# Another order of the value products in a windowed-attention section: four phases of 320 columns, heads alternating between the two halves

## The chip, the cores and the metric

One core of one Trainium2 chip runs the whole program in one launch. The metric is device time in microseconds (us). Several runs of the kernel before were timed; one more execution was recorded by the hardware profiler, and its page and trace are what is read here. Engine names are those of the profile: PE is TensorE's matmul, PEld its weight load, DVE is VectorE, ACT is ScalarE, POOL is GpSimd, SP is SyncE.

## The reference

A gate mixes an attention branch and a feed-forward branch over the same input, with 2048 positions and 512 features:

```
def A(x, wqkv, wo):                        # x: 1 x 2048 x 512
    H = 32; Dh = 16; W = 256
    q, k, v = split(x @ wqkv)              # 32 heads of 16
    scores = einsum("bhqd,bhkd->bhqk", q, k) * Dh ** -0.5
    mask = (i - j >= 0) & (i - j < W)      # causal, window of 256
    p = softmax(where(mask, scores, -1e9))
    return einsum("bhqk,bhkd->bhqd", p, v) @ wo
def B(x, w_gate, w_up, w_down):            # 512 -> 1792 -> 512
    return (silu(x @ w_gate) * (x @ w_up)) @ w_down
g = sigmoid((x * gate_w).sum(-1, keepdims=True))
out = g * A(x) + (1 - g) * B(x)
```

## The kernel before

The 32 heads are worked on in G = 8 groups g of four heads j. Positions come in 16 blocks of 128 (the block of keys is called kb) and in 4 chunks c of 512 columns (the queries). The program has three stretches: projections and first scores (to about 95 us), the attention groups with the feed-forward's gate and up products between them (about 95 to 603 us), and the down products and the output (to the end).

In the attention stretch the loop at L694 runs over slots t, each with four steps hd. A step issues, in a fixed order, one matmul of the next group's scores (`stage1`, L302, reduced to a row maximum on DVE at L304), one transposed score of this group (`stage2`, L344, turned by ACT's Exp at L346 into the probabilities `pt`, which POOL masks at L348 and L351), and six feed-forward matmuls (L252). Once in four slots, in the step hd == 1 of part 0, it calls `av(ag, c)` (L715), the section that is changed, and then `finish(ag, c)`, whose first instruction is ACT's copy at L383, followed by DVE's sum and transposes. All of it is ordered by hand: every engine takes its instructions in the order of the program, and waits are put in where data or a buffer is needed.

A section `av(g, c)` makes, for one group and one chunk, the products of values and probabilities and, by a column of ones, their sums. Both operands are fp32; one matmul call of the program becomes two weight loads and two matmul passes on PE. A block of 128 keys is split by `HALVES` into its first and last 64 keys, so that TensorE's rows are used as two halves h: half 0 reads partitions 0 to 63 and sums into one PSUM tile (`pb`, or `pa` at the very end), half 1 reads partitions 64 to 127 and sums into another (`ps`). The four heads write 32 partitions each. So eight places of the array, two halves by four heads, can work beside each other.

What a block gives to a chunk depends on where it lies. With m the block's number relative to the chunk's first block, the columns of the product are:

| m | -2 | -1 | 0 | 1 | 2 | 3 | sum |
|---|---|---|---|---|---|---|---|
| half 0 | 64 | 192 | 320 | 320 | 256 | 128 | 1280 |
| half 1 | 128 | 256 | 320 | 320 | 192 | 64 | 1280 |

The first chunk (c = 0) has no blocks -2 and -1, so its sums are 1024 and 896. `SEQUENCE` (L326) is the order of the pairs (h, m); the loop below it issues, for each pair, the four heads one after another:

```
for n, (h, kb) in enumerate(todo):
    ...
    for j in range(4):
        nc.tensor.matmul(AV[g, c][h][32 * j:32 * j + 32, q0 - c * CH:q1 - c * CH],
        ...
                         start=n == at[h][0], stop=n == at[h][-1], skip_group_check=True)
```

A section therefore has 12 blocks of four heads, 48 matmuls; the first chunk's has 8 blocks, 32 matmuls. There are 24 sections of the first kind (8 groups by 3 chunks) and 8 of the second.

Of the kernel before, what the change touches and what calls it, by code (L numbers as in the profile page):

```python
# [16 lines left out]
P = 128  # L17
# [3 lines left out]
CH = 512  # L21
# [15 lines left out]
def gated_mix(ctx, tc, xT, xn, wqk, wv, wo, wgu, wd, gw, outT):  # L37
# [4 lines left out]
    nc = tc.nc  # L42
# [158 lines left out]
    with ExitStack() as A:  # L201
# [121 lines left out]
        VG, PT, AV = {}, {}, {}  # L323


        SEQUENCE = ((0, 0), (1, -2), (1, -1), (0, 1), (1, 0), (0, -2), (0, -1), (1, 1), (0, 2), (1, 2), (0, 3), (1, 3))  # L326

        def load_v(n):

# [26 lines left out]
        def av(g, c):  # L356


            AV[g, c] = (pp.tile([P, CH], F32, name="pb" if 4 * g + c + 1 < G * NB // 4 else "pa"),
                        ps1.tile([P, CH], F32, name="ps1") if 4 * g + c + 1 >= 4 * (G - 1) else ps2.tile([P, CH], F32, name="ps2"))  # L360

            todo = [(h, 4 * c + m) for h, m in SEQUENCE if 4 * c + m >= 0]
            at = [[n for n, (o, _) in enumerate(todo) if o == h] for h in range(2)]
            for n, (h, kb) in enumerate(todo):
                o, k0 = HALVES[h], kb * P + 64 * h
                q0, q1 = max(k0, c * CH), min(k0 + W + 64, c * CH + CH)
                for j in range(4):
                    nc.tensor.matmul(AV[g, c][h][32 * j:32 * j + 32, q0 - c * CH:q1 - c * CH],  # L368
                                     VG[4 * g + kb // 4][o, kb % 4, 17 * j:17 * j + 32],
                                     PT[g, kb, j // 2][o, j % 2, q0 - kb * P:q1 - kb * P],  # L370
                                     start=n == at[h][0], stop=n == at[h][-1], skip_group_check=True)

        AB = []

# [142 lines left out]
        for n, turn in enumerate(turns):  # L517
            for m, _ in enumerate(turn, 3 * NK * n):
                at = [max(0, i - wait) * 2 * NB // (total - wait) for i in (m, m + 1)]
# [174 lines left out]
        for t in range(G * NB + 1):  # L694
            g, i = divmod(t, NB)
            d, part = divmod(t, NSLOT)
            if part == 0:
                turns = unit(t) if t < G * NB else [iter(())] * NSLOT
            s1 = stage1(g + 1, i) if t < g7 else iter(())
            s2 = stage2(g, i) if t < G * NB else iter(())  # L700
            for hd in range(4):
                run(s1, 1)
                if t < g7:
                    run(s2, 1)
                elif hd % 2 == 0:
                    run(s2, 2)
                run(turns[part], 3)
                for f in AT.pop((t, hd), ()):
                    f()
                if (part, hd) in ((0, 2), (1, 1), (1, 3), (2, 1)):  # L710
                    run(FIN, 1)
                if hd == 1 and part == 0:
                    if t:
                        ag, c = divmod(d - 1, NCH)
                        av(ag, c)  # L715
                        FIN = finish(ag, c)
                        run(FIN, 1)
            if i in (7, 15) and g + 1 < G:
                later(t + 1, 2, lambda g=g, i=i: put_max(g + 1, i // 8))
            if t >= 10 and t % 4 == 2 and t + 6 < G * NB:  # L720
                load_v((t + 6) // 4)
# [6 lines left out]
    with ExitStack() as B:  # L728
# [7 lines left out]
        def column():  # L736
            return hp.tile([P, CH], F32, name="sg", bufs=4)
# [185 lines left out]
        def bank(p, pr):  # L923
            if p in (1, 6, 7, 4):
                pool, name = ((ps1, "ps1"), (ps2, "ps2"))[pr]
            else:
                pool, name = pp, ("pa", "pb")[pr]
            if name not in BANK or BANK[name][0] != p and p in (5, 2, 3):
                BANK[name] = p, [pool.tile([P, CH], F32, name=name) for _ in range(2)]
            return BANK[name][1]  # L930
# [73 lines left out]
        at = {e: n for n, e in enumerate(ITEMS)}  # L1004
# [7 lines left out]
        for j in range(2 * NP):  # L1012
            two = divmod(j, 2)
            n = WO + j
# [20 lines left out]
        for i in range(NP):  # L1035
            n = WO + 57 + 4 * (i // 2) + i % 2 - (i == 6)
# [22 lines left out]
        two, t, part, rest = bank(4, 1), *(column() for _ in range(3))  # L1059
# [46 lines left out]
```

## Time and profile before

| what | value |
|---|---|
| timed runs, median of 3 | 806.68 us |
| lowest, highest of them | 806.06, 806.93 us |
| the profiled execution's own time | 805.95 us |
| its span, first to last instruction | 804.2 us |
| mean granted TensorE clock | 0.999 |
| PE busy | 796.1 us, 99% of the span |
| matmuls of the section's line, L368, two records for each | 2816 records |

The page lists busy time by engine, then 40 equal slices of the span, the DMA queues, the chain of work that ended last, and the costliest groups of instructions. A group's row reads: line, engine, operation, tile written and tiles read, rows and columns of the array used, sizes, count; then busy time in us and the mean length of one in ns. A timeline's row gives the start and the length in us of a run of equal instructions, of which the count stands behind the x; the length reaches from the first one's start to the last one's end. Matmuls are pipelined, so a matmul's record is longer than the time until the next one starts on the same place of the array.

### The profile page before, as it was taken

What the parts mean: (1) busy time and instruction counts of PE and PEld (TensorE: products, weight loads), DVE (VectorE), ACT (ScalarE), POOL (GpSimd) and SP (SyncE); (2) the same over time, 40 slices, a digit from 0 to 9 for tenths busy, and PEclk for the clock granted to TensorE, in tenths of its full rate; (3) what the DMA queues carried; (4) which work ended last, traced back from release to release, by engine and by line L of the source; (5) the groups of instructions that cost most, each with busy time, mean ns of one, the idle gap of its engine ahead of it and who ended that gap; (6) DMA issues with size and microseconds to landing.
All of it is one profiled execution on the core that took longest, in us unless ns stands there. A gap on an engine that the chain in (4) does not pass through costs nothing.

```text
span 804.2 us, 21513 instructions
## 1 busy us (share of the span) xinstructions
PE 796.1 (99%) x8251; PEld 688.0 (86%) x8251; DVE 628.4 (78%) x1685; ACT 432.3 (54%) x882; POOL 344.8 (43%) x647
## 2 busy tenths in 40 slices
PE   8999999999999999999999999999999999999997
PEld 6888999889889889888988988888888888888886
DVE  5397687868887787878777878888675478899896
ACT  6412656666566566555666556645643235554642
POOL 7721546564545546544656464545740111000212
PEclk9999999999999999999999999999999999999999
DMA  8575415434252453352434516334627898728435
GB/s 300 167 205 159 140 58 133 122 110 136 70 164 77 117 167 92 113 148 68 134 107 140 151 40 205 130 103 167 206 95 237 270 335 307 289 78 270 95 54 104
DMA packets 61963, 121.88 MB, mean 152 GB/s; under 512 B 10852, under 2 KB 19556, under 8 KB 61604
## 3 DMA queue, kind: packets, MB, share of 16 engines
q1 hardware_dynamic: 54756, 99.27, 40.1%
q0 software_dynamic: 7104, 21.24, 9.0%
q8 instruction: 65, 1.06, 0.6%
q14 instruction: 38, 0.31, 0.1%
HBM read 55.97 MB, written 39.34 MB: 119 GB/s over the span
## 4 chain that ended last, share of the span: by engine, by line
PE 97%; DVE 2%; DMA 1%; issue 0%; SPq 0%; ACT 0%
PE pb L252 24%; PE pa L252 24%; PE ps L302 6%; PE ps L368 5%; PE ps L344 4%; PE ps L90 4%; PE ps L88 4%; PE ps L89 4%; PE pb L368 4%; PE pb L232 2%; PE pa L232 2%; PE pb L90 2%; PE pa L90 2%; PE pa L88 2%; PE pb L88 2%; PE pb L89 2%
## 5 line engine op out<-in xcount | busy, mean ns | idle before, releaser
L304 DVE CUSTOM_DVE_ANT_0 ps<-ps,mask 128x384 f32<-128x384 f32 (+2 forms) x512 | 268.8, 540 | 99.9 <-PE ps L344 51.5
L346 ACT ACTIVATE pt<-ps 128x384 f32<-128x384 f32 (+2 forms) x512 | 238.3, 475 | 131.2 <-PE ps L302 71.2
L348 POOL TENSOR_SCALAR_AFFINE_SELECT pt<-pt 128x256 f32<-128x256 f32 x256 | 108.4, 424 | 200.2 <-ACT pt L346 199.1
L344 PE MATMUL ps<-q,k 64*128 64x384 f32 (+2 forms) x512 | 161.5, 333 | 0.0
L302 PE MATMUL ps<-k,q 63*128 63x384 f32 (+2 forms) x512 | 159.4, 331 | 0.5 <-DVE mx L304 0.5
L252 PE MATMUL pb<-xhi,wh 64*128 64x512 f32 x512 | 117.2, 395 | 0.1
L252 PE MATMUL pb<-xlo,wh 64*128 64x512 f32 x512 | 115.6, 391 | 0.0
L252 PE MATMUL pb<-xhi,wl 64*128 64x512 f32 x512 | 115.4, 392 | 0.0
L252 PE MATMUL pa<-xhi,wh 64*128 64x512 f32 x512 | 114.5, 393 | 0.0
L252 PE MATMUL pa<-xlo,wh 64*128 64x512 f32 x512 | 113.2, 391 | 0.0
L252 PE MATMUL pa<-xhi,wl 64*128 64x512 f32 x512 | 113.2, 391 | 0.0
L302 PEld LDWEIGHTS ps<-k,q 63*128 63x128 f32 x512 | 88.7, 185 | 15.7 <-DVE mx L304 3.1
L351 POOL TENSOR_SCALAR_AFFINE_SELECT pt<-pt 128x256 f32<-128x256 f32 x224 | 99.2, 443 | 0.0
L344 PEld LDWEIGHTS ps<-q,k 64*128 64x128 f32 x512 | 90.7, 184 | 4.3 <-ACT pt L346 0.4
L368 PE MATMUL ps<-pt,vg 64*32 64x320 f32 (+4 forms) x1408 | 74.2, 346 | 0.0
L304 DVE DVE_READ_ACCUMULATOR2_ANT mx<- 128x1 f32 x512 | 71.7, 140 | 0.0
L368 PE MATMUL pb<-pt,vg 64*32 64x320 f32 (+2 forms) x1360 | 69.9, 349 | 0.0
L252 PEld LDWEIGHTS pb<-xhi,wh 64*128 64x128 f32 x512 | 62.3, 185 | 6.5 <-DVE o L385 0.8
L252 PEld LDWEIGHTS pb<-xhi,wl 64*128 64x128 f32 x512 | 62.0, 184 | 5.3
L252 PEld LDWEIGHTS pa<-xhi,wl 64*128 64x128 f32 x512 | 60.0, 184 | 5.8
L252 PEld LDWEIGHTS pa<-xhi,wh 64*128 64x128 f32 x512 | 60.1, 186 | 3.7
L252 PEld LDWEIGHTS pb<-xlo,wh 64*128 64x128 f32 x512 | 62.1, 185 | 0.4
(305 smaller groups left out, 1611.3 us busy)
## 6 DMA issues: line engine op xcount, KB each, us to landing
kept_h<-ev SPq DMA_DIRECT2D x52, 256.0 KB
od<-o POOLq DMA_DIRECT2D x32, 256.0 KB, 3.7
raw<-wgu SPq DMA_DIRECT2D x28, 256.0 KB
q<-xhi SPq DMA_DIRECT2D x56, 128.0 KB
k<-xhi SPq DMA_DIRECT2D x56, 128.0 KB
outT<-sg POOLq DMA_DIRECT2D x28, 256.0 KB, 4.1
vd<-vs POOLq DMA_DIRECT2D x8, 672.0 KB, 4.7
vg<-vd SPq DMA_DIRECT2D x32, 168.0 KB
```

What stands on the lines that cost most here:

```text
L88: nc.tensor.matmul(ps, lh, rh, start=start and i == 0, stop=False, skip_group_check=skip)
L89: nc.tensor.matmul(ps, lh, rl, start=False, stop=False, skip_group_check=skip)
L90: nc.tensor.matmul(ps, ll, rh, start=False, stop=stop and i == n - 1, skip_group_check=skip)
L232: nc.tensor.matmul(ps, w, x, start=n == 0, stop=n == len(todo) - 1)
L252: mm = nc.tensor.matmul(ps[me], w[r], x[r], start=not second and i == 0, stop=bool(second) and i == n - 1)
L302: nc.tensor.matmul(ps[:, :n], QT[g % 2][pr][r, q0:q0 + P], KT[g % 2][pr][r, k0:k0 + n], start=True, stop=True)
L304: mx = nc.vector.tensor_tensor_reduce(out=ps[:, :n], in0=ps[:, :n], in1=mask[:, 3 * P - n:], scale=1.0, scalar=NEG, op0=ALU.add, op1=ALU.m ...
L344: nc.tensor.matmul(ps[:, :n], KT[g % 2][pr][r, k0:k0 + P], QT[g % 2][pr][r, k0:k0 + n], start=True, stop=True)
L346: BEHIND.append(nc.scalar.activation(pt[:, j, :n], ps[:, :n], AF.Exp, scale=SCALE))
L348: nc.gpsimd.affine_select(out=pt[:, :, :P], in_=pt[:, :, :P], pattern=[[0, 2], [1, P]], compare_op=ALU.is_ge, fill=0.0, base=0, channel_mu ...
L351: nc.gpsimd.affine_select(out=pt[:, :, 2 * P:], in_=pt[:, :, 2 * P:], pattern=[[0, 2], [-1, P]], compare_op=ALU.is_ge, fill=0.0, base=-1, ...
L368: nc.tensor.matmul(AV[g, c][h][32 * j:32 * j + 32, q0 - c * CH:q1 - c * CH], VG[4 * g + kb // 4][o, kb % 4, 17 * j:17 * j + 32], PT[g, kb, ...
```

## The change

The order in which a section's matmuls are issued is replaced. Blocks now come in four phases. In each, a block of 320 columns on one half stands beside two blocks of the other half that have 320 columns together: (0,0) beside (1,-2) and (1,2); (1,0) beside (0,-2) and (0,2); (0,1) beside (1,-1) and (1,3); (1,1) beside (0,-1) and (0,3). Where a phase begins, two blocks are issued together, the heads alternating: head 0 of the one, head 0 of the other, head 1 of the one, and so on; the phase's third block follows with its four heads. The first chunk goes through m = 0 to 3 with both halves' blocks alternating in the same way. The start flag is now set for the first four matmuls of a half (one for each head) and the stop flag for its last four. The number of matmuls, their sizes and their operands stay the same.

```diff
-        SEQUENCE = ((0, 0), (1, -2), (1, -1), (0, 1), (1, 0), (0, -2), (0, -1), (1, 1), (0, 2), (1, 2), (0, 3), (1, 3))
+        SEQUENCE = (((0, 0), (1, -2)), ((1, 2),), ((1, 0), (0, -2)), ((0, 2),),
+                    ((0, 1), (1, -1)), ((1, 3),), ((1, 1), (0, -1)), ((0, 3),))
+        FIRST_CHUNK = [((0, m), (1, m)) for m in range(4)]
...
-            todo = [(h, 4 * c + m) for h, m in SEQUENCE if 4 * c + m >= 0]
-            at = [[n for n, (o, _) in enumerate(todo) if o == h] for h in range(2)]
-            for n, (h, kb) in enumerate(todo):
+            todo = [(h, 4 * c + m, j) for two in (SEQUENCE if c else FIRST_CHUNK) for j in range(4) for h, m in two]
+            at = [[n for n, (o, _, j) in enumerate(todo) if o == h] for h in range(2)]
+            for n, (h, kb, j) in enumerate(todo):
                 o, k0 = HALVES[h], kb * P + 64 * h
                 q0, q1 = max(k0, c * CH), min(k0 + W + 64, c * CH + CH)
-                for j in range(4):
-                    nc.tensor.matmul(AV[g, c][h][32 * j:32 * j + 32, q0 - c * CH:q1 - c * CH],
-                                     VG[4 * g + kb // 4][o, kb % 4, 17 * j:17 * j + 32],
-                                     PT[g, kb, j // 2][o, j % 2, q0 - kb * P:q1 - kb * P],
-                                     start=n == at[h][0], stop=n == at[h][-1], skip_group_check=True)
+                nc.tensor.matmul(AV[g, c][h][32 * j:32 * j + 32, q0 - c * CH:q1 - c * CH],
+                                 VG[4 * g + kb // 4][o, kb % 4, 17 * j:17 * j + 32],
+                                 PT[g, kb, j // 2][o, j % 2, q0 - kb * P:q1 - kb * P],
+                                 start=n in at[h][:4], stop=n in at[h][-4:], skip_group_check=True)
```

## The prediction, as recorded before the change was run

> **What bounds the kernel now.** First the page, for whether TensorE sets the time at all.
>
> ```profile
> span 804.2 us, 21513 instructions
> ...
> PE 796.1 (99%) x8251; PEld 688.0 (86%) x8251; DVE 628.4 (78%) x1685; ACT 432.3 (54%) x882; POOL 344.8 (43%) x647
> ...
> PEclk9999999999999999999999999999999999999999
> ...
> PE 97%; DVE 2%; DMA 1%; issue 0%; SPq 0%; ACT 0%
> ```
>
> PE is busy all the way, carries 97% of the chain that ended last, and its clock is granted in full in every slice. Next the stretch that holds nearly all sections, by windows, and PE's waits from 95 to 600 us.
>
> ```profile
> core 0: us, PE busy (x) PEld busy (x) DVE busy (x) ACT busy (x) POOL busy (x), PEclk, DMA share, GB/s
> 95.00:555.00 460.00, 459.41 (x6036) 405.88 (x6034) 372.31 (x1164) 277.00 (x597) 248.16 (x501) 1.00 0.39 119
> ```
>
> ```profile
> PE ps L302 <- DVE mx L304: 0.5, 2, 0.2
> ```
>
> PE is idle for 0.54 us of 460, and waits for DVE for 0.5 us. So whatever a section gains or loses on PE moves the end by as much, but for at most 0.5 us that a later PE could save in waits. A busy PE isn't a PE at its peak, though: the question is how well the eight places (two halves, four heads) are filled inside a section. For that I read one section closely, the last chunk of the fourth group, in order of time.
>
> ```profile
> 210.88 0.47 PE L368 MATMUL pb<-pt,vg 64*32 64x320 f32 x4
> 210.90 0.64 PE L368 MATMUL ps<-pt,vg 64*32 64x128 f32 x12
> 211.17 0.45 PE L368 MATMUL pb<-pt,vg 64*32 64x320 f32 x4
> 211.36 0.40 PE L368 MATMUL ps<-pt,vg 64*32 64x256 f32 x4
> 211.44 0.45 PE L368 MATMUL pb<-pt,vg 64*32 64x320 f32 x4
> 211.58 0.54 PE L368 MATMUL ps<-pt,vg 64*32 64x320 f32 x4
> 211.71 0.45 PE L368 MATMUL pb<-pt,vg 64*32 64x320 f32 x4
> ...
> 211.98 0.45 PE L368 MATMUL pb<-pt,vg 64*32 64x64 f32 x12
> ...
> 212.96 0.29 PE L368 MATMUL pb<-pt,vg 64*32 64x128 f32 x4
> 212.98 0.38 PE L368 MATMUL ps<-pt,vg 64*32 64x64 f32 x8
> 213.29 0.32 PE L302 MATMUL ps<-k,q 63*128 63x128 f32 x1
> ```
>
> The section takes 213.29 - 210.88 = 2.41 us. Half 0 (pb) runs its passes of 320 columns at 210.88, 211.17, 211.44, 211.71, 211.98: 0.27 us each, 0.29 the first, whose weights weren't loaded ahead (0.02 more). That is 0.84 ns a column, so about 0.22 us for 256 columns, 0.16 for 192, 0.11 for 128 and 0.06 for 64. Both halves have 1280 columns in two passes, 8 x 0.27 = 2.16 us.
>
> ```profile
> L368 PE MATMUL ps<-pt,vg 64*32 64x64 f32 x8 | 0.4, 216 | 0.0
> ```
>
> A 64-column record is 0.22 us long and its columns take 0.06. Half 0's last pass starts by 212.96 + 0.29 - 0.27 = 212.98 and is through its 128 columns at 213.09; half 1's last starts at 212.98 + 0.38 - 0.22 = 213.14 and is through at 213.20. Counted from 210.88 that is 2.21 and 2.32: half 1 ends the section, and 0.09 us later the next matmul starts. Why is half 1 late? Its row at 211.58 is 0.54 long where half 0's are 0.45: the four heads, elsewhere 0.02 apart, are spread over 0.1. The weight loads say more.
>
> ```profile
> 211.36 0.11 PEld L368 LDWEIGHTS ps<-pt,vg 64*32 64x32 f32 x1
> 211.44 0.13 PEld L368 LDWEIGHTS pb<-pt,vg 64*32 64x32 f32 x4
> 211.58 0.22 PEld L368 LDWEIGHTS ps<-pt,vg 64*32 64x32 f32 x7
> ```
>
> Loads for a following pass come four at a time as soon as the present pass starts; but at 211.36, for block (1,0), one comes alone. The other heads' matmuls start late. Two narrow windows give the times:
>
> ```profile
> 211.64 0.48 PE L368 MATMUL ps<-pt,vg 64*32 64x320 f32 x3
> ...
> 211.17 0.43 PE L368 MATMUL pb<-pt,vg 64*32 64x320 f32 x1
> ```
>
> In this kind of section (1,0) is the fifth block, so its head 0 is the 17th matmul, and the 18th starts at 211.64, 0.05 behind its turn (211.58 plus 0.01). The first matmul's second pass starts at 211.17 and ends at 211.60, 0.04 before. So 16 matmuls seem to be in PE's queue at once, and the 18th comes in when the first has ended. What a matmul is in the queue:
>
> ```profile
> L368 PE MATMUL ps<-pt,vg x1408: 216/360/454, 95.8 to 601.1; 64*32 64x320 f32 x64, 64*32 64x192 f32 x40, 64*32 64x128 f32 x24, 64*32 64x256 f32 x24
> L368 PE MATMUL pb<-pt,vg x1360: 216/376/454, 95.7 to 587.6; 64*32 64x320 f32 x71, 64*32 64x256 f32 x36, 64*32 64x128 f32 x35, 64*32 64x192 f32 x27
> L368 PE MATMUL pa<-pt,vg x48: 216/350/453, 598.8 to 600.9; 64*32 64x320 f32 x16, 64*32 64x64 f32 x8, 64*32 64x192 f32 x8, 64*32 64x256 f32 x8
> ```
>
> 2816 records for 24 x 48 + 8 x 32 = 1408 matmuls: two loads and two passes each, so 16 matmuls are 64 instructions. The 17th gets its first load in time (211.36) because the first matmul's first pass has then ended. A first chunk's section tests the rule on another block:
>
> ```profile
> 292.70 0.47 PE L368 MATMUL pb<-pt,vg 64*32 64x320 f32 x4
> ...
> 294.38 0.27 PE L368 MATMUL ps<-pt,vg 64*32 64x64 f32 x4
> 294.58 0.44 PE L302 MATMUL ps<-k,q 63*128 63x384 f32 x1
> ```
>
> ```profile
> 293.54 0.43 PE L368 MATMUL pb<-pt,vg 64*32 64x320 f32 x1
> ...
> 294.00 0.36 PE L368 MATMUL ps<-pt,vg 64*32 64x192 f32 x2
> 294.02 0.32 PE L368 MATMUL ps<-pt,vg 64*32 64x192 f32 x1
> 294.04 0.34 PE L368 MATMUL ps<-pt,vg 64*32 64x192 f32 x1
> ```
>
> Here the late ones are heads 1 to 3 of (1,2), the 22nd to 24th matmuls, from 294.00. The fifth matmul, (0,1) on head 0, starts its second pass at 293.54 and ends it at 293.97, 0.03 before. Same rule, other block: **the k-th matmul comes in 0.03 to 0.04 after the (k-17)th has ended, never before the one ahead of it in the program**, and further ones follow 0.02 apart. A 320-column pass ends 0.43 after its start, so a place can be empty for 0.16 + 0.03 although its next matmul stands in the program.
>
> **The change part by part.** The number of matmuls, their widths, start flags and loads are as before; only the order moves. All 32 sections are on the path.
>
> *Data wanted earlier.* (1,2) and (1,3) move forward; the newest probabilities must be there.
>
> ```profile
> 208.97 0.76 POOL L348 TENSOR_SCALAR_AFFINE_SELECT pt<-pt 128x256 f32<-128x256 f32 x2
> 210.88 0.41 POOL L348 TENSOR_SCALAR_AFFINE_SELECT pt<-pt 128x256 f32<-128x256 f32 x1 [1.14 <-ACT pt L346]
> ...
> 213.42 0.59 ACT L383 COPY o<-ps 128x512 f32<-128x512 f32 x1 [1.03 <-PE ps L368]
> 213.91 0.50 ACT L346 ACTIVATE pt<-ps 128x384 f32<-128x384 f32 x1
> ```
>
> (The two pairs are of two views, POOL's and ACT's.) The last masking of this chunk's blocks ends at 209.73, 1.15 us ahead of the section; POOL's next, at 210.88, is for the block after it. Nothing lost. Behind the section ACT's copy waits for its end, with Exp queued behind; both move with PE's next scores, so their distances stay. Nothing.
>
> *First chunks, 8 sections.* Blocks alternate pair by pair, eight matmuls a pair. The 17th is (0,2) on head 0, due after four passes, at 1.10; the first ends at 0.29 + 0.43 = 0.72. The 25th is due at 1.54; the ninth, (0,1), ends at 0.83 + 0.43 = 1.26. Nobody is late. Half 0 sets the end: 1.10 + 2 x 0.22 + 2 x 0.11 = 1.76, and 0.04 for head 3, since eight first loads instead of four go ahead of it (before, four took 0.02): 1.80. Now the end is 294.38 + 0.27 - 0.22 + 0.06 = 294.49, 1.79. Nothing.
>
> *The other 24 sections.* Times from the first matmul, in us. Numbering: 1 to 8 are (0,0) and (1,-2) by turns, 9 to 12 (1,2), 13 to 20 (1,0) and (0,-2) by turns, 21 to 24 (0,2), 25 to 32 (0,1) and (1,-1), 33 to 36 (1,3), 37 to 44 (1,1) and (0,-1), 45 to 48 (0,3).
> - First to second phase. The 18th, (0,-2) on head 2, is due at 0.03 + 0.56 = 0.59. The first matmul ends at 0.72, so it comes at 0.76: 0.17 late. The 20th, the same on head 3, comes at 0.79, due 0.60: 0.19 late. And (0,2), 21 to 24, comes behind these: head 0 at 0.81, due 0.67. So all of half 0 is 0.14 to 0.2 behind; head 3 starts (0,2) at 0.93.
> - Second to third. The 30th, (1,-1) on head 2, waits for the 13th, (1,0) on head 0: passes at 0.58 and 0.85, end 1.28. It comes at 1.31, due 1.14. Half 1's heads 2 and 3 are now late by as much as half 0's.
> - Third to fourth. The 42nd, (0,-1) on head 2, waits for the 25th, (0,1) on head 0. That head had (0,2) at 0.81 and, with a load not made ahead, 1.05, and (0,1) at 1.27 and 1.54: end 1.97. So the 42nd comes at 2.00 and the 44th, on head 3, at 2.03, where head 3 was due at 0.93 + 2 x 0.22 + 2 x 0.27 = 1.91: 0.12 late again.
> - The end: 2.03 + 0.02 + 2 x 0.16 + 2 x 0.11 = 2.59, where now it is 2.32.
>
> So 0.27 us a section. The old order's own lateness (0.1 of half 1) is counted in it, being part of the 2.32. **Sum:** 24 x 0.27 + 8 x 0 = 6.5; less some of the 0.5 us of PE's waits on DVE, of which I take 0.2 back: 6.3 us. On the profiled execution's own 805.95 us (span 804.2 and 1.75 around it) that is 812.2; it lies 0.73 under the median of the runs, 806.68, so the median becomes 813.0. Bounds of this one unknown, a section's change: below, no place is ever late, 8 x 0.27 + 0.02 + 0.04 = 2.22, a gain of 0.10; above, one head loses at all three changes of phase, 0.19 + 0.17 + 0.12 = 0.48 on that 2.22, so 0.38 more than now. I take 0.27, since two sections of different order bear the rule out to 0.01.
>
> One rule of the Trainium skill speaks for the change: TensorEngine Tiling (Array Packing), Key Properties, says that tiles work independently and can load and multiply in parallel. The trace agrees within the queue (pb and ps overlap) and not beyond it: head 1 of half 1 stood empty until 211.64. By that rule alone the section would come to the lower bound.
>
> **The rivals.** *Faster:* the places are free of each other, and what delays heads 1 to 3 now is something else than the queue. Then a section takes 0.10 less, 24 x 0.10 = 2.4: 804.3. For it: the phases are of equal width. Against it: different blocks are late in the two kinds, each 0.03 to 0.04 behind the end of the matmul 17 places earlier. It decides if the 18th matmul starts by 0.6. 0.10. This is where that page's rule would lead.
>
> *Late once:* heads 0 and 1, running ahead by 0.2, end early enough that later changes of phase cost nothing. Head 3 then ends at 2.22 + 0.21 = 2.43, 24 x 0.11 = 2.6: 809.3. For it: the heads do drift apart. Against it: (0,2) is held back on every head. 0.10.
>
> *Late three times on one head:* 24 x 0.38 = 9.1: 815.8. 0.06.
>
> *No change:* the lateness is as large as what half 1 loses now, 0.1 of 2.22. That needs a refill well before the end of a matmul, against both rows. 806.7, 0.06.
>
> **How the numbers follow.** The forecast, slower by 0.27 a section, has 0.68; its own range, 0.18 to 0.35 a section (4.3 to 8.4 us), is 811.0 to 815.1. A measurement can tell 0.2%, 1.6 us, from no change. Faster 0.10, same 0.06, slower 0.68 + 0.10 + 0.06 = 0.84. The range takes in the slower cases, from under 809.3 to over 815.8, with half a microsecond of the runs' own spread: 808.8 to 816.2; 0.16 lies outside.
>
> **What would show it.** Right: first-chunk sections stay 1.88 us from first matmul to the next score, the others go from 2.41 to about 2.68; in the loads' timeline of such a section heads 0 and 1 of (0,-2) load ahead and heads 2 and 3 only about 0.75 after the start, and rows of (0,-2) and (1,1) are stretched to 0.2 or more over the heads; matmuls of L368 still have 2816 records, and the stretch from 95 to 603 us grows by 6 us while those before and after keep theirs. Wrong: a section of 2.3 us or less with all four heads 0.02 to 0.04 apart (the queue isn't the limit), or a wait of PE on POOL or ACT inside a section (data wanted too early).

## The result, and the profile after

| | us |
|---|---|
| before, median of 6 runs | 806.36 (805.34 to 806.93) |
| changed, median of 6 runs | 812.34 (811.50 to 813.17) |
| ratio, changed to before | 1.0079, 95% interval 1.0069 to 1.0090 |

The change makes the kernel 6.0 us slower; 6.3 were forecast. Source lines below `FIRST_CHUNK` have moved: the section is now L369, the next scores L302 and L346.

The page of the changed kernel, its span and engines:

```profile
span 811.0 us, 21536 instructions
...
PE 803.7 (99%) x8251; PEld 693.5 (86%) x8251; DVE 627.5 (77%) x1685; ACT 432.6 (53%) x882; POOL 347.1 (43%) x647
...
PE 94%; DVE 2%; DMA 2%; SPq 0%; issue 0%; ACT 0%; POOL 0%; DVEq 0%
```

PE has the same 8251 matmuls and is busy 7.6 us longer; DVE, ACT and POOL work as long as before to within 2.3 us. Windows of the changed kernel, then of the one before, cut at the first section's start and at the last one's end (the columns are those of the prediction's windows):

```profile
0.00:95.37 95.37, 93.53 (x662) 78.86 (x662) 62.91 (x191) 42.36 (x78) 48.43 (x69) 1.00 0.66 202
95.37:608.02 512.65, 511.25 (x6706) 449.73 (x6705) 405.98 (x1239) 301.45 (x655) 277.31 (x549) 1.00 0.39 120
608.02:811.00 202.98, 198.96 (x888) 164.94 (x885) 158.61 (x256) 88.78 (x149) 21.36 (x30) 1.00 0.67 203
```

```profile
0.00:95.70 95.70, 92.15 (x662) 78.03 (x662) 62.52 (x191) 42.40 (x78) 48.07 (x69) 1.00 0.66 201
95.70:601.25 505.55, 504.96 (x6705) 445.03 (x6705) 407.25 (x1239) 301.11 (x655) 275.38 (x549) 1.00 0.40 121
601.25:804.20 202.95, 198.97 (x889) 164.99 (x885) 158.60 (x256) 88.77 (x149) 21.35 (x30) 1.00 0.67 204
```

The span's growth lies in the stretch with the sections: 512.65 for 505.55. Of PE's 7.6 busy us 6.3 are there; the other 1.4 are in the first stretch, which did not get longer (95.37 for 95.70). The section that the prediction reads is the last chunk of the second group (it calls it the fourth's by mistake; nothing hangs on it). PE's timeline of the same section now:

```profile
211.97 0.45 PE L369 MATMUL pb<-pt,vg 64*32 64x320 f32 x1
211.98 0.29 PE L369 MATMUL ps<-pt,vg 64*32 64x128 f32 x1
...
212.26 0.47 PE L369 MATMUL pb<-pt,vg 64*32 64x320 f32 x4
...
212.75 0.45 PE L369 MATMUL ps<-pt,vg 64*32 64x320 f32 x1
212.76 0.43 PE L369 MATMUL pb<-pt,vg 64*32 64x64 f32 x4
...
213.28 0.40 PE L369 MATMUL ps<-pt,vg 64*32 64x256 f32 x1
...
214.00 0.38 PE L369 MATMUL pb<-pt,vg 64*32 64x192 f32 x3
...
214.31 0.41 PE L369 MATMUL pb<-pt,vg 64*32 64x128 f32 x4
214.66 0.32 PE L302 MATMUL ps<-k,q 63*128 63x128 f32 x1
```

From 211.97 to 214.66 are 2.69 us (2.68 by the unrounded times), against 2.41 or 2.42. The heads alternate at the start (pb at 211.97, ps at 211.98) and then drift apart: where the old order has rows of four, here single heads stand between those of other blocks. The weight loads around the first change of phase:

```profile
212.54 0.11 PEld L369 LDWEIGHTS pb<-pt,vg 64*32 64x32 f32 x1
...
212.55 0.11 PEld L369 LDWEIGHTS pb<-pt,vg 64*32 64x32 f32 x1
...
212.72 0.10 PEld L369 LDWEIGHTS pb<-pt,vg 64*32 64x32 f32 x1
212.74 0.10 PEld L369 LDWEIGHTS ps<-pt,vg 64*32 64x32 f32 x1
212.75 0.11 PEld L369 LDWEIGHTS pb<-pt,vg 64*32 64x32 f32 x2
```

Heads 0 and 1 of (0,-2) load at 212.54 and 212.55, 0.57 after the start. Head 2 loads only at 212.72, 0.75 after it, and head 3 of (1,0) at 212.74: the first matmul's second pass, at 212.26, ends 0.43 later at 212.69. The first chunk of the fourth group, the other section that the prediction reads:

```profile
294.93 0.45 PE L369 MATMUL pb<-pt,vg 64*32 64x320 f32 x1
...
296.36 0.31 PE L369 MATMUL ps<-pt,vg 64*32 64x64 f32 x8
296.46 0.42 PE L369 MATMUL pb<-pt,vg 64*32 64x128 f32 x8
296.81 0.44 PE L302 MATMUL ps<-k,q 63*128 63x384 f32 x1
```

It takes 1.88, as before. Half 0 ends it: its last pass starts at 296.46 + 0.42 - 0.27 = 296.61, half 1's at 296.36 + 0.31 - 0.22 = 296.45. In the whole trace the 24 longer sections take 2.68 each and the 8 first chunks' 1.88; L369 has 2816 records, as L368 had.

### The profile page after: what moved, and what is told of

Same layout as the page of the kernel before. It is cut to its first block, busy times and chain, and to the rows that moved or that the text cites. A ratio compares the mean times of both kernels' runs of the same rounds, so it can differ in the third digit from the quotient of the medians.

```text
span 811.0 us, 21536 instructions
## 1 busy us (share of the span) xinstructions
PE 803.7 (99%) x8251; PEld 693.5 (86%) x8251; DVE 627.5 (77%) x1685; ACT 432.6 (53%) x882; POOL 347.1 (43%) x647
## 4 chain that ended last, share of the span: by engine, by line
PE 94%; DVE 2%; DMA 2%; SPq 0%; issue 0%; ACT 0%; POOL 0%; DVEq 0%
PE pb L252 23%; PE pa L252 23%; PE ps L302 7%; PE pb L369 5%; PE ps L346 4%; PE ps L89 4%; PE ps L90 4%; PE ps L88 4%; PE ps L369 4%; PE pb L232 2%; PE pb L89 2%; PE pa L89 2%; PE pb L90 2%; PE pa L90 2%; PE pb L88 2%; PE pa L88 2%
## 5 line engine op out<-in xcount | busy, mean ns | idle before, releaser
L350 POOL TENSOR_SCALAR_AFFINE_SELECT pt<-pt 128x256 f32<-128x256 f32 x256 | 110.4, 432 | 204.8 <-ACT pt L348 203.7
L346 PE MATMUL ps<-q,k 64*128 64x384 f32 (+2 forms) x512 | 161.6, 333 | 0.0
L302 PE MATMUL ps<-k,q 63*128 63x384 f32 (+2 forms) x512 | 159.4, 331 | 0.5 <-DVE mx L304 0.5
L302 PEld LDWEIGHTS ps<-k,q 63*128 63x128 f32 x512 | 88.7, 185 | 18.2 <-issue 5.7
L353 POOL TENSOR_SCALAR_AFFINE_SELECT pt<-pt 128x256 f32<-128x256 f32 x224 | 99.4, 444 | 0.0
L346 PEld LDWEIGHTS ps<-q,k 64*128 64x128 f32 x512 | 90.6, 184 | 4.7 <-issue 0.8
L369 PE MATMUL ps<-pt,vg 64*32 64x320 f32 (+4 forms) x1408 | 79.3, 346 | 0.0
L369 PE MATMUL pb<-pt,vg 64*32 64x320 f32 (+3 forms) x1360 | 78.9, 351 | 0.0
L369 PEld LDWEIGHTS pb<-pt,vg 64*32 64x32 f32 x1360 | 49.9, 106 | 18.1 <-DVE mx L304 5.2
```

What stands on the lines that cost most here:

```text
L302: nc.tensor.matmul(ps[:, :n], QT[g % 2][pr][r, q0:q0 + P], KT[g % 2][pr][r, k0:k0 + n], start=True, stop=True)
L346: nc.tensor.matmul(ps[:, :n], KT[g % 2][pr][r, k0:k0 + P], QT[g % 2][pr][r, k0:k0 + n], start=True, stop=True)
L350: nc.gpsimd.affine_select(out=pt[:, :, :P], in_=pt[:, :, :P], pattern=[[0, 2], [1, P]], compare_op=ALU.is_ge, fill=0.0, base=0, channel_mu ...
L353: nc.gpsimd.affine_select(out=pt[:, :, 2 * P:], in_=pt[:, :, 2 * P:], pattern=[[0, 2], [-1, P]], compare_op=ALU.is_ge, fill=0.0, base=-1, ...
```

## The experiments

Two things were open: whether it is the queue that makes heads late and not the alternation or the phases as such, and whether an order can be found that is never late. The first two edits and the last are against the changed kernel, the other four against the kernel before. The first two runs, the split and the heads outermost ran once and are compared with one run of the kernel before on the same chip, 805.06 us; the other three are compared with its 19 runs there, median 805.62. Those 19 reach from 804.50 to 807.18, so where a kernel ran once, a difference of 1 or 2 us says little, and the section's length in the trace decides.

**The old blocks, heads alternating.**

```diff
-        SEQUENCE = (((0, 0), (1, -2)), ((1, 2),), ((1, 0), (0, -2)), ((0, 2),),
-                    ((0, 1), (1, -1)), ((1, 3),), ((1, 1), (0, -1)), ((0, 3),))
+        SEQUENCE = (((0, 0), (1, -2)), ((1, -1), (0, 1)), ((1, 0), (0, -2)),
+                    ((0, -1), (1, 1)), ((0, 2), (1, 2)), ((0, 3), (1, 3)))
```

> The old order of blocks, but two blocks at a time with their heads alternating (first chunks as in the changed kernel). Queue theory (the k-th matmul comes in 0.03 us after the (k-17)th has ended): a section of 48 matmuls from 2.42 to 2.47 us, a first chunk's stays 1.88; 806.4 + 24 x 0.05 = 807.6. Rival, the alternation of heads itself is what costs: the 24 sections come near the changed kernel's 2.68, 812.5. Rival, free places: 2.33, 804.

Measured 806.53, 1.5 more than the kernel before. The section of the second group's last chunk, first and next matmul:

```profile
210.56 0.45 PE L369 MATMUL pb<-pt,vg 64*32 64x320 f32 x1
...
213.03 0.32 PE L302 MATMUL ps<-k,q 63*128 63x128 f32 x1
```

2.47, as the queue theory has it. 21 of the 24 take that; three take 2.49 to 2.51, and why was not traced. Alternating heads cost 0.05 a section, not 0.27: the alternation isn't what made the change slow.

**The new blocks, heads not alternating.**

```diff
-        SEQUENCE = (((0, 0), (1, -2)), ((1, 2),), ((1, 0), (0, -2)), ((0, 2),),
-                    ((0, 1), (1, -1)), ((1, 3),), ((1, 1), (0, -1)), ((0, 3),))
-        FIRST_CHUNK = [((0, m), (1, m)) for m in range(4)]
+        SEQUENCE = (((0, 0),), ((1, -2),), ((1, 2),), ((1, 0),), ((0, -2),), ((0, 2),),
+                    ((0, 1),), ((1, -1),), ((1, 3),), ((1, 1),), ((0, -1),), ((0, 3),))
+        FIRST_CHUNK = [((h, m),) for m in range(4) for h in range(2)]
```

> The new order of blocks, but four heads of a block together, not alternating with another block. Queue theory: still late at the changes of phase and a little more so, as the next phase's second block comes in behind all heads of its first: 2.73 us instead of 2.68; a first chunk's section 1.86; 806.4 + 24 x 0.32 - 0.1 = 813.9. Rival, the alternation costs: with it gone the sections fall back to 2.42 or less, 806.4 or less.

Measured 812.75, 7.7 more than the kernel before, with the same section at

```profile
211.46 0.47 PE L369 MATMUL pb<-pt,vg 64*32 64x320 f32 x4
...
214.19 0.32 PE L302 MATMUL ps<-k,q 63*128 63x128 f32 x1
```

2.73. So the order of the blocks costs all of it, and alternating them had won 0.05 back. The rival falls in both runs.

**One swap in the old order.**

```diff
-        SEQUENCE = ((0, 0), (1, -2), (1, -1), (0, 1), (1, 0), (0, -2), (0, -1), (1, 1), (0, 2), (1, 2), (0, 3), (1, 3))
+        SEQUENCE = ((0, -2), (1, -2), (1, -1), (0, 1), (1, 0), (0, 0), (0, -1), (1, 1), (0, 2), (1, 2), (0, 3), (1, 3))
```

> The old order with (0,0) and (0,-2) in each other's place, nothing else. Queue theory: the first matmul, now 64 columns wide, ends before the 18th is due, so no head is late: sections of 2.33 us instead of 2.42 and 1.86 instead of 1.88, 24 x 0.09 + 8 x 0.02 = 2.3 us less than the kernel before on the same chip (0.3%). If (1,0) is late for a reason of its own (its data, its bank), nothing changes.

Measured 804.33, median of 11 runs; ratio to before 0.9984, interval 0.9975 to 0.9993. Faster, by 1.3 and not 2.3 us. The same section:

```profile
209.82 0.26 PE L368 MATMUL pb<-pt,vg 64*32 64x64 f32 x4
...
212.15 0.33 PE L302 MATMUL ps<-k,q 63*128 63x128 f32 x1
```

That is 2.33 (2.32 unrounded), and 16 of the 24 have it; the first chunks' take 1.86. But eight take 2.36 to 2.41. One of them, the third chunk of the second group:

```profile
193.08 0.26 PE L368 MATMUL pb<-pt,vg 64*32 64x64 f32 x4
...
193.25 0.43 PE L368 MATMUL pb<-pt,vg 64*32 64x320 f32 x1
```

The view of the line in that section:

```profile
L368 PEldq EVENT_SEMAPHORE  x1: 51/51/51, 193.1 to 193.1; - x1
```

Half 0's second block, (0,1), starts 0.17 after the first (0.18 by the unrounded times); in the sections of 2.32 it starts at 0.14. Exactly the eight late sections have a semaphore wait of 51 ns of PE's sequencer in their first 0.17 us; in the others it comes well before the section or not at all. That this wait makes them late rests on the match of eight with eight; what it waits for was not traced. Together the eight lose 0.4 us of the 1.0 that is missing from the 2.3; the rest is within the interval, which reaches from 0.6 to 2.0 us.

**The same with wide blocks split.**

```diff
...
+                cuts = (q0, q0 + 160, q1) if q1 - q0 == 320 else (q0, q1)
+                for i, (a, b) in enumerate(zip(cuts, cuts[1:])):
+                    for j in range(4):
+                        nc.tensor.matmul(AV[g, c][h][32 * j:32 * j + 32, a - c * CH:b - c * CH],
...
```

> The old order with (0,0) and (0,-2) in each other's place, and every block of 320 columns made as two matmuls of 160: the same columns and the same order of work, but 64 matmuls in place of 48. Queue theory with 64 instructions: 2.63 us for the 24 sections and 1.96 for the 8, 812.0. If the queue holds a fixed amount of work (columns) and not a number of instructions, or if the places are free: 2.34 and 1.87, 804.3.

Measured 810.54, 5.5 more than the kernel before. The same section as above, and a first chunk's:

```profile
211.10 0.26 PE L370 MATMUL pb<-pt,vg 64*32 64x64 f32 x4
...
213.73 0.32 PE L302 MATMUL ps<-k,q 63*128 63x128 f32 x1
...
293.84 0.34 PE L370 MATMUL pb<-pt,vg 64*32 64x160 f32 x4
...
295.80 0.44 PE L302 MATMUL ps<-k,q 63*128 63x384 f32 x1
```

2.63 and 1.96, both as expected. The columns and their order are those of the swap, with its 2.33 and 1.86: what fills up is a number of instructions, not an amount of work. Which of them it counts is not told by these runs: passes leave it one by one (in the kernel before, the 17th matmul's first load comes at 211.36, and the first matmul's first pass ends at 210.88 + 0.45 = 211.33), but every matmul here has two loads and two passes, so 32 passes fit as well as 64 instructions. The 51 ns wait falls into the same eight sections, 0.07 to 0.08 after their start, and they take 2.63 like the others: here it costs nothing.

**Heads outermost.** The old order within a head, head after head.

```diff
-            for n, (h, kb) in enumerate(todo):
+            for j, n, (h, kb) in [(j, n, x) for j in range(4) for n, x in enumerate(todo)]:
...
```

> The old order of blocks within a head, but head 0's twelve blocks first, then head 1's and so on. Every place gets the same matmuls in the same order as before. Queue theory: only some 16 matmuls, one head's and a part of the next, can be in work at once, so a section takes 4.83 us and a first chunk's 3.80; 806.4 + 24 x 2.41 + 8 x 1.92 = 879.6. Free places: 2.33, no slower than before.

Measured 954.44, 149.4 more than before, where the queue of 64 accounts for 73. Its sections take 7.57 and 5.20, not 4.83 and 3.80. So the theory was incomplete. Where does head 1 begin? A section's start, and 1.76 us later:

```profile
114.75 0.45 PE L367 MATMUL pb<-pt,vg 64*32 64x320 f32 x1
...
116.51 0.32 PE L367 MATMUL ps<-pt,vg 64*32 64x192 f32 x1
116.51 0.45 PE L367 MATMUL pb<-pt,vg 64*32 64x320 f32 x1
116.52 0.29 PE L367 MATMUL ps<-pt,vg 64*32 64x128 f32 x1
...
116.72 0.27 PE L367 MATMUL pb<-pt,vg 64*32 64x128 f32 x1
```

Head 1's first matmul (pb, 320) is the section's 13th, and a queue of 16 would have had it from the start. It comes at 116.51, in the moment in which head 0 on half 1 starts (1,2)'s first pass and has three passes left: the second of (1,2) and two of (1,3). From that a second rule: a place takes three waiting passes beside the one under way, and a pass that doesn't fit holds up all that stand behind it in the program. Each head then begins 1.76 after the one before, and three such steps, the last head's own 2.2 and the 0.09 to the next matmul make the 7.57. The lengths of the other orders were met without this rule.

**Halves outermost,** a test of that rule on another order.

```diff
-        SEQUENCE = ((0, 0), (1, -2), (1, -1), (0, 1), (1, 0), (0, -2), (0, -1), (1, 1), (0, 2), (1, 2), (0, 3), (1, 3))
+        SEQUENCE = ((0, 0), (0, 1), (0, -2), (0, -1), (0, 2), (0, 3), (1, -2), (1, -1), (1, 0), (1, 1), (1, 2), (1, 3))
```

> All of half 0's blocks first, then all of half 1's. Two rules: the 64 instructions alone give 3.79 us for the 24 sections and 2.42 for the 8. With the second rule that the run with the heads outermost showed (a place takes three waiting passes beside the one under way, and what is behind in the program waits until the next fits): 3.93 and 2.81. So 839.7 + 4.3 by the first alone, 24 x 1.51 + 8 x 0.93 = 43.7 more than before, 849, by both.

Measured 846.20 in a single run, 40.6 more than the kernel before and between the two forecasts, so the time doesn't decide; sections of 3.86 and 2.77 do, and their starts. The starts of a first chunk's section and of one of the others:

```profile
95.16 1.50 PE L368 MATMUL pb<-pt,vg 64*32 64x320 f32 x20
96.28 0.47 PE L368 MATMUL ps<-pt,vg 64*32 64x320 f32 x4
...
219.24 1.93 PE L368 MATMUL pb<-pt,vg 64*32 64x320 f32 x36
220.80 0.42 PE L368 MATMUL ps<-pt,vg 64*32 64x128 f32 x8
```

The first row covers four passes of (0,0) and (0,1) on four heads and the first pass of (0,2), whose last record, 0.38 long, starts at 95.16 + 1.50 - 0.38 = 96.28: three passes are left on that place, and half 1 begins, at 1.12. By the queue alone its first matmul, the 17th, would have come in at 0.76. In the other section the first row ends with (0,2)'s first passes too, the last at 219.24 + 1.93 - 0.38 = 220.79, and half 1 begins at 220.80, 1.56 after the start, where the queue alone would let it in 0.04 after the eighth matmul, (0,1) on head 3, has ended: at about 0.85 + 0.43 + 0.04 = 1.32. So the second rule decides in both. The 2.77 is near its 2.81 and far from 2.42; the 3.86 lies between 3.79 and 3.93, since the working behind the expectation had half 1 begin 0.04 later than it does and head follow head by 0.016 instead of 0.007, together 0.07.

**The phases kept, narrow, wide, narrow.**

```diff
-        SEQUENCE = (((0, 0), (1, -2)), ((1, 2),), ((1, 0), (0, -2)), ((0, 2),),
-                    ((0, 1), (1, -1)), ((1, 3),), ((1, 1), (0, -1)), ((0, 3),))
-        FIRST_CHUNK = [((0, m), (1, m)) for m in range(4)]
+        SEQUENCE = (((0, -2),), ((1, 0),), ((0, 2),), ((0, -1),), ((1, 1),), ((0, 3),),
+                    ((1, 2),), ((0, 0),), ((1, -2),), ((1, -1),), ((0, 1),), ((1, 3),))
+        FIRST_CHUNK = [((h, m),) for m in range(4) for h in range(2)]
```

> The four phases of the change are kept (a block of 320 columns beside two narrow ones of the other half), but the wide block is issued between the two narrow ones, four heads of a block together, and the phases come in another order; first chunks by blocks, half by half. Queue theory: a section 2.33 us and a first chunk's 1.86, about 2.1 us less than the kernel before. If phases of 320 columns cost by themselves: between the kernel before and the changed one.

Measured 803.62, median of 9 runs; ratio to before 0.9978, interval 0.9968 to 0.9988. It is faster than the kernel before by 2.0 us, about what was expected.

```profile
209.88 0.26 PE L369 MATMUL pb<-pt,vg 64*32 64x64 f32 x4
209.91 0.47 PE L369 MATMUL ps<-pt,vg 64*32 64x320 f32 x4
...
212.21 0.32 PE L302 MATMUL ps<-k,q 63*128 63x128 f32 x1
```

All 24 sections take 2.33 and the first chunks' 1.86. The same phases as in the change, in another order within and among them, cost 0.35 us less each. Phases of equal width are no loss as such; what was lost lay in what stands 17 matmuls apart.

## Why the prediction was right, step by step

- *PE sets the time, so a section's change moves the end.* Shown: 24 sections by 0.27 make 6.4 us of the 7.1 that the stretch grew in the profiled execution, and the six runs' medians differ by 6.0. What remains there is mostly one wait, which the waits of PE in the two traces tell apart:

```profile
PE pb L252 <- DVE o L388: 0.9, 1, 0.9
PE ps L302 <- DVE mx L304: 0.5, 2, 0.2
```

  The second row is that of before. The first is new: PE waits once, at 564.92, for `finish` of a first chunk. DVE's timeline tells why DVE is late with that:

```profile
561.43 1.81 DVE L192 TENSOR_TENSOR ev<-ev 128x256 f32<-128x256 f32 x4 [1.67 <-DMA ev<-wd]
```

  It had waited 1.67 us for weights from a DMA. In the run of nearly the same speed, the new blocks with heads not alternating, PE waits 0.3 us for `finish`, and with the wide blocks split not at all, so it isn't put down to the order.
- *0.2 us would come back from PE's waits for DVE.* Not borne out: they are 0.5 as before. It is a small term, within the spread of the runs, which is 1.6 us before and 1.7 after; that the forecast met the time to 0.3 is in part luck.
- *The rule of 17.* Each place in the sum was met. The prediction had (0,-2) on head 2 at 0.76 and the same block on head 3 at 0.79; the loads stand at 0.75 and the row of head 3 at 212.76 - 211.97 = 0.79. (1,-1) on head 2 was to come at 1.31: 213.28 - 211.97 = 1.31. (0,-1) on head 3, at 2.03: 214.00 - 211.97 = 2.03. The ends used here are those of the profile's records, which it models. The section's end, 2.59: the last row's last pass starts at 214.31 + 0.41 - 0.27 = 214.45 and is through its 128 columns at 214.56, 2.59 after the start.
- *First chunks stay.* 1.88 and 1.88. Half 0 sets the end, as forecast. The 0.02 that eight first loads cost its last head shows in the run with these blocks not alternating: 1.86.
- *Data wanted earlier costs nothing.* Shown: PE's list has no wait on POOL or ACT.
- *The rivals.* "Faster" needed free places: the runs with heads and halves outermost, where every place has the same matmuls as before and a section takes 7.57 and 3.86, exclude it. "Late once" falls with the matches at 1.31 and 2.03. "Late three times on one head" would have made the section 0.38 longer, "no change" not at all; it is 0.27 longer. The rival tested beside these, that alternating heads costs, falls with the first two runs.

What the prediction did not know is the second rule, three waiting passes a place. It didn't matter for this change, whose steps are all met without it; it doubled the loss where an order put a head's blocks back to back.

The Trainium skill's page TensorE: Matmul & The Clock Gate, Architectural detail, gives TensorE's queue as 64 deep. The trace agrees, if loads count as well as passes: 16 matmuls of four instructions. Its section The mechanism says that matmuls start and end strictly in the order of the program; here the first matmul's second pass starts at 212.26, after the first passes of seven other matmuls, and with the heads outermost the 13th matmul starts at 116.51, the 11th, (0,3) of head 0, at 116.72; so on different places they don't. And TensorEngine Tiling (Array Packing), Key Properties, by which tiles work independently, holds only for what has come through that queue.

## What to carry to other kernels

Where small matmuls work side by side in parts of the array, count the instructions between a matmul and the next one of the same place: with two loads and two passes for an fp32 product, 16 matmuls fill the queue, and a wide one at its head keeps the others out until its record ends, 0.16 us after its columns are through. Put narrow blocks ahead of wide ones, as in the two orders that were faster here, and keep the places' turns even in instructions, not only in columns; balanced widths alone made this kernel slower. Then look at the weight loads in the trace: rows of one where there should be four are the sign.

## What the runs showed of the hardware beyond that

- A place of the array takes three waiting passes beside the running one; the next holds up everything behind it in the program (7.57 us a section with heads outermost, 3.86 with halves outermost, 2.33 in the best order, for the same work).
- A semaphore wait of 51 ns in PE's sequencer in a section's first 0.17 us goes with 0.04 to 0.08 us more for the section in the order with one swap, and with nothing more in the same order with wide blocks split.
- The 24 longer sections of the changed kernel all take 2.68 us, from 2.682 to 2.684, so a single trace separates orders that differ by 0.02 us a section, 0.5 us in all, which timed runs of this kernel don't.
